# Weights of a step scaled or summed at the end of the step in front, their words made ahead of the second block's probabilities, and the squares spread over four steps

## The chip, the cores and the metric

The kernel runs on one core of one Trainium2 chip. The metric is the device time of one launch in microseconds (us); the time before is the median of three runs. A kernel's profile is one further execution, recorded by the hardware profiler.

## What is computed

The reference mixes two branches of the same 2048 tokens of width 576 with a gate per token:

```python
x = A_x
g = _sigmoid((x * gate_w).sum(-1, keepdims=True))
a = _A_ref(x, A_wq, A_wk, A_wv, A_wo, A_beta)      # 32 heads of 18, 4 segments of 512 tokens
b = (_gelu(x @ w_gate) * (x @ w_up)) @ w_down       # hidden width 4608
return g * a + (1 - g) * b
```

In `_A_ref` each head has, per segment, a causal softmax over 512x512 logits times the values, mixed with a recall from a memory that the segments in front have written. Matrix products are made of two 16-bit words per number, a high word and a low word (the rest that the high word leaves), so that one product of the reference is three on TensorE.

## The kernel before

**Stages.** First the projections q, k, v and the memory recalls are made (to about 205 us). Then come 72 steps `v`, two for each of the 36 slices of 128 hidden columns `f = v // 2`; a slice is taken for the first 1024 tokens at even `v` and for the second 1024 at odd `v`. Last comes the product with wo. Steps 5 to 65 are `paired_step`: beside the feed-forward work of its slice and token half, each does one head of one half of the tokens in attention (`k = v - 2`), as two blocks, `a = 2k` and `b = 2k + 1`. Four steps make a group `fb = v // 4`, with `i4 = v % 4`.

**Order.** TensorE (PE), ScalarE (ACT), VectorE (DVE) and GpSimd (POOL) run their instructions in the order in which the program text issues them (`manual_schedule`). Only the queue of the DMA issues (SP) is ordered by the framework. So an instruction that waits holds up all that stands behind it on its engine.

**A paired step on TensorE** is, in order: the first product into V (`first_product`, words at S3), the product A11 into X, two chains of the group in front (`late(0, 2)`; a chain is six products of 288 columns in `down`, L1051, taken into `acc` by VectorE, L1059), values of the even block (L1005), A22 and G4 into V, `late(2, 4)`, S2 into Y, `late(4, 6)`, in steps with `i4 == 1` the tiny product of `scales` (L234), values of the odd block, `late(6, 8)`, S1, G4, the low rests (L1102), the eight score products of both blocks (L948), A12 and U4 into X, S4 and UG into Y.

**Banks.** The chains, the product of `scales` and four of the score products take turns in two PSUM banks called dn. A new tile takes the bank of the tile before last, and its first instruction waits until that tile's last reader is done. `scales` reads and writes its dn tile with six small VectorE instructions, L236 to L244.

**Weights.** A slice's raw fp32 weights are loaded to `raw` (gate and up) and `rawd` (down). Their sums of squares are made on ScalarE (`squares`, L85), `scales(fb + 1)` turns these into scales on VectorE, and `scales_out` (L250 to L258) finishes them on GpSimd. GpSimd then scales raw weights in place (`scale_g`, L278, `scale_d`, L317) or, a step later, forms their sums and differences (`sums_g`, L299 to L303). `weights_first(fb, i4)` issues these: scaling at `i4` 0 and 2, sums at 1 and 3, and `scale_d` at 2 and 3 as well. ScalarE makes the high words (`weights_high`, L309 and L321) and GpSimd the low words (`weights_low`, L313 and L325). The words of a step's half of a slice are thus used from the next step or the one behind it on; those made at `i4 == 3` are first needed by the first product of the next step.

**Probabilities.** A score piece is taken from PSUM by VectorE with the mask and its row maximum (`put`, L954) into `pf`. `powers` makes the exponentials on ScalarE (L971, L974), `pair_rows` the high words on ScalarE (L984) and the low words on GpSimd (L985, two instructions to a block), and `turn_rows` transposes them by DMA (L991). Block `a` goes through this at the end of its own step, block `b` in the middle of the next step, where its remaining pieces are also taken. `pf` has two buffers, so a piece of block `b` waits until the low words of block `b` of the step in front are made.

**The hidden half.** VectorE adds the partial sums (L1242, L1244), ScalarE applies gelu (L1081; its table has to be loaded again after exponentials), VectorE multiplies (`hidden`, L1073), ScalarE and GpSimd make the words `hh` (L1077, L1078).

Of the kernel before, what the change touches and what calls it, by code (L numbers as in the profile page):

```python
# [18 lines left out]
P = 128  # L19
# [23 lines left out]
def kernel(ctx: ExitStack, tc: tile.TileContext, xs, wqk, wv, wo, wgu, wd, beta, out):  # L43
# [846 lines left out]
    with tc.tile_pool(name="keep", bufs=2, side="right", reuse_waits="tile") as kp, ExitStack() as tail:  # L890
# [226 lines left out]
        def weights_high(fb, i4):  # L1117
            n0 = 2 * fb
            high_g(n0 + 1 + i4 // 2, i4 % 2)
            if i4 >= 2:  # L1120
                high_d(n0 + i4 - 2)

        def weights_low(fb, i4):
            n0 = 2 * fb
            low_g(n0 + 1 + i4 // 2, i4 % 2)
            if i4 >= 2:
                low_d(n0 + i4 - 2)
# [16 lines left out]
        def act_squares(v):  # L1144

            fb, i4 = divmod(v, 4)
            todo = {0: ((fb + 1, 2 * fb, 2),),
                    1: ((fb + 1, 2 * fb + 3, 0), (fb + 1, 2 * fb + 3, 1), (fb + 1, 2 * fb + 1, 2)),
                    2: ((fb + 2, 2 * fb + 4, 0), (fb + 2, 2 * fb + 4, 1))}
            todo = todo.get(i4, ()) if fb else ()  # L1150
            if v == 4:
                todo += (2, 4, 0), (2, 4, 1)
            for b, f, i in todo:
                squares(b, f, i, act_square)
# [22 lines left out]
        def paired_step(v):  # L1177

            f, p = divmod(v, 2)
            fb, i4 = divmod(v, 4)  # L1180
            c, e = 2 * p, 2 * p + 1
            k = v - LAG
            a, b = 2 * k, 2 * k + 1
            late = lambda i, j: chains(fb - 1, range(8 * i4 + i, 8 * i4 + j))
            put = puts.pop(2 * k - 1)
            done = (k - 5) // 4 if i4 == 3 and 0 <= (k - 5) // 4 < H // 2 else None
            low = (k - 6) // 4 if i4 == 0 and 0 <= (k - 6) // 4 < H // 2 - 1 else None
            x1, x2_, t = x16[c], x16[e], xt[p]
            X, Y = bank("G"), bank("U")
            if ends:  # L1190
                end_pair([lambda i=i: put(i) for i in (2, 3)])
            V, g1 = first_product(v), gl_tile()
            dve.tensor_copy(g1, V)
            act_squares(v)
            product(X, f, A11, x1, 0, 4, True)
            put(0)
            dve.tensor_copy(Y, X)
            put(1)
            put(3)
            late(0, 2)  # L1200
            values(2 * k - 4)
            weights_first(fb, i4)
            powers(2 * k - 1)
            pair_rows(2 * k - 1, 0)
            pair_rows(2 * k - 1, 1)
            turn_rows(2 * k - 1)
            weights_high(fb, i4)
            weights_low(fb, i4)
            weights_load(fb, i4)
            product(V, f, A22, x2_, 0, 4)  # L1210
            rest(V, f, G4, x1, (0,))
            late(2, 4)
            if low is not None:
                result_low(low)
            product(Y, f, S2, t, 4, 6)
            g0 = gl_tile()
            dve.tensor_copy(g0, Y)
            late(4, 6)
            if i4 == 1:
                scales(fb + 1)  # L1220
                scales_out(fb + 1)
            values(2 * k - 3)
            normalize(k - 2)
            late(6, 8)
            if i4 == 3:
                load_v(fb + 1)
            product(Y, f, S1, t, 0, 2)
            rest(Y, f, G4, x2_, (0,))
            low_rests(f, (V, G4, x1), (Y, G4, x2_))
            (one, put1), (two, put2) = score(a), score(b)  # L1230
            s0, s1, d0, d1, o = bank("st", 2), bank("st", 2), bank("dn", 2), bank("dn", 2), bank("pv")
            one(0, 0, d1)
            one(1, 64, o[:, : 3 * P])
            one(3, 64, o[:, 3 * P :])
            two(0, 0, s0)
            one(2, 64, d0[:, : 2 * P])
            two(2, 64, d0[:, 2 * P :])
            low_rests(f, (X, U4, x1))
            two(1, 64, s1[:, : 3 * P])
            two(3, 64, s1[:, 3 * P :])  # L1240
            puts[b] = put2
            dve.tensor_tensor(g1, Y, g1, OP.add)  # L1242
            gelu(f, e, g1, g1)
            dve.tensor_tensor(g0, V, g0, OP.add)  # L1244
            gelu(f, c, g0, g0)
            put1(2)
            put2(2)
            product(X, f, A12, x1, 2, 6)
            rest(X, f, U4, x1, (0,))
            hidden(f, c, X, g0)  # L1250
            hidden_pair(f, c, g0)
            put1(0)
            put1(1)
            put1(3)
            product(Y, f, S4, x2_, 2, 6)
            rest(Y, f, UG, x2_)
            hidden(f, e, Y, g1)
            powers(a)
            pair_rows(a, 0)
            pair_rows(a, 1)  # L1260
            turn_rows(a)
            if done is not None:
                result_high(done)
            hidden_pair(f, e, g1)
            load_head(k + 2)
            if i4 == 2:
                load_ob(fb)
# [320 lines left out]
        LAG = 2  # L1588
# [68 lines left out]
```

## Time and profile before

| | |
|---|---|
| median of 3 runs | 1590.53 us (1590.24 to 1590.97) |
| the profiled execution's own time | 1590.79 us |
| its span, first to last instruction | 1589.1 us |
| paired steps, first to last, by the window asked for | 276 to 1406 us |
| in this window: PE busy | 1109.87 of 1130.00 us |
| ACT, POOL, DVE busy there | 941.31, 943.27, 832.42 us |
| granted TensorE clock | 1.00 of full |

A line of the profile has engine, source line, operation, output and inputs; in the timeline the first two numbers are start and length in us, neighbours of one kind are merged (`x6`), and a bracket gives how long the engine had been idle before and what released it. The length of a PE line holds the way through the array, so two matmuls of 512 columns lie about 0.22 us apart though each is shown with 0.38. PE's busy time is therefore no measure of gaps: they are read from starts.

### The profile page before, as it was taken

The page shows a single profiled execution, that of the slowest core. Times are in us where ns is not written, and L with a number is a line of the kernel's source. Part 1 is how long each engine was busy: PE and PEld are TensorE (multiplying, and loading weights), DVE is VectorE, ACT ScalarE, POOL GpSimd, SP SyncE. Part 2 cuts the span into 40 slices and gives each one's busy share as a digit, 9 for nine tenths or more (in the row PEclk, how much of TensorE's full clock was granted, in tenths as well). Part 3 has the DMA queues.
Part 4 walks back from the last instruction along what each step waited for, and adds up shares of the span by engine and source line. Part 5 has one row for each costly group of instructions (what it writes and reads, how often), then busy time and mean ns, then how long its engine had stood idle before and what let it go on. Part 6 is the DMA issues. An engine that isn't in the chain of part 4 may idle for free.

```text
span 1589.1 us, 32678 instructions
## 1 busy us (share of the span) xinstructions
PE 1563.7 (98%) x11902; PEld 937.8 (59%) x11902; DVE 1158.2 (73%) x2995; ACT 1179.7 (74%) x1973; POOL 1225.9 (77%) x1164
## 2 busy tenths in 40 slices
PE   9999999999999999999999999999999999999999
PEld 5665654555555555556555555555555555555577
DVE  6688876777777686777777777777786777775766
ACT  6667648888888787878787888888788888884310
POOL 3445767878888888788888778888878888887774
PEclk9999999999999999999999999999999999999999
DMA  6633346687878696869687778878686879745153
GB/s 222 217 124 115 138 143 107 116 136 121 135 121 146 114 155 118 141 121 141 121 137 130 135 140 123 138 130 140 119 158 121 140 127 144 124 80 142 40 142 98
DMA packets 472305, 209.00 MB, mean 132 GB/s; under 512 B 427600, under 2 KB 437072, under 8 KB 471632
## 3 DMA queue, kind: packets, MB, share of 16 engines
q1 hardware_dynamic: 472144, 206.92, 68.1%
q8 instruction: 93, 1.52, 0.4%
q14 instruction: 68, 0.56, 0.1%
HBM read 90.99 MB, written 27.26 MB: 74 GB/s over the span
## 4 chain that ended last, share of the span: by engine, by line
PE 37%; POOL 26%; ACT 23%; DVE 7%; issue 5%; DMA 2%; SPq 1%; POOLq 0%; ACTq 0%; DVEq 0%
POOL ph L985 8%; PE dn L1051 7%; ACT pf L974 6%; POOL raw L278 6%; PE U L1091 4%; ACT gl L1081 4%; ACT L974 4%; ACT L1081 4%; DVE pf L954 4%; PE G L1091 3%; PE V L1091 3%; POOL rawd L317 3%; POOL hh L1078 3%; PE st L333 3%; DVE gl L1073 2%
## 5 line engine op out<-in xcount | busy, mean ns | idle before, releaser
L985 POOL TENSOR_TENSOR ph<-pf,ph 128x512 f16<-128x512 f32 (+1 forms) x256 | 353.3, 1401 | 181.0 <-ACT ph L984 177.1
L1091 PEld LDWEIGHTS <-pairg 128*128 128x128 f16 x3024 | 283.1, 98 | 335.5 <-POOL pairg L313 27.5
L1051 PE MATMUL dn<-paird,hh 128*128 128x288 f16 x3408 | 465.9, 286 | 0.0
L1051 PEld LDWEIGHTS <-hh 128*128 128x128 f16 x3456 | 333.0, 98 | 124.6 <-DVE pb L244 0.3
L1059 DVE SCALAR_TENSOR_TENSOR acc<-dn,ev,acc 128x288 f32<-128x288 f32 x536 | 264.5, 514 | 120.1 <-PE dn L1051 119.7
L974 ACT ACTIVATE pf<-pf,mb,esc 128x512 f32<-128x512 f32 (+3 forms) x512 | 293.0, 643 | 7.0 <-POOL hh L1078 0.4
L1091 PE MATMUL G<-x,pairg 128*128 128x512 f16 x864 | 212.0, 380 | 0.5 <-DVE gl L1073 0.4
L1091 PE MATMUL U<-xt,pairg 128*128 128x512 f16 x864 | 210.0, 379 | 0.0
L1078 POOL TENSOR_TENSOR hh<-gl,hh 128x512 f16<-128x512 f32 x144 | 174.4, 1213 | 14.7 <-ACT hh L1077 14.7
L313 POOL TENSOR_TENSOR pairg<-raw,pairg 128x640 f16<-128x640 f32 (+2 forms) x144 | 174.4, 1232 | 4.0 <-ACT pairg L309 4.0
L984 ACT ACTIVATE ph<-pf 128x512 f16<-128x512 f32 (+1 forms) x256 | 172.4, 721 | 0.0
L954 DVE CUSTOM_DVE_ANT_0 pf<-dn,mask 128x256 f32<-128x256 f32 (+1 forms) x195 | 95.8, 497 | 87.7 <-POOL ph L985 83.6
L309 ACT ACTIVATE pairg<-raw 128x640 f16<-128x640 f32 (+2 forms) x144 | 89.8, 650 | 78.5 <-POOL raw L303 48.6
L1077 ACT ACTIVATE hh<-gl 128x512 f16<-128x512 f32 x144 | 89.6, 623 | 74.0 <-DVE gl L1073 73.8
L278 POOL TENSOR_SCALAR raw<-raw,sc 128x640 f32<-128x640 f32 x72 | 135.5, 1894 | 0.0
L1091 PE MATMUL V<-xt,pairg 128*128 128x512 f16 x432 | 107.7, 380 | 20.1 <-POOL pairg L313 20.1
L1081 ACT ACTIVATE gl<-gl,sc 128x512 f32<-128x512 f32 x144 | 96.5, 715 | 32.3 <-DVE gl L1383 20.0
L1091 PE MATMUL U<-x,pairg 128*128 128x512 f16 x432 | 107.3, 379 | 0.0
L1091 PE MATMUL V<-x,pairg 128*128 128x512 f16 x432 | 104.8, 378 | 0.0
L954 DVE CUSTOM_DVE_ANT_0 pf<-st,mask 128x512 f32<-128x512 f32 (+2 forms) x195 | 95.1, 512 | 0.0
L1005 PEld LDWEIGHTS <-pt 128*128 128x128 f16 x2560 | 83.3, 96 | 5.4
L1005 PE MATMUL pv<-vt,pt 128*128 128x37 f16 x2560 | 84.3, 179 | 0.0
(311 smaller groups left out, 2671.2 us busy)
## 6 DMA issues: line engine op xcount, KB each, us to landing
raw<-in_wgu_dram SPq DMA_DIRECT2D x36, 640.0 KB
rawd<-in_wd_dram SPq DMA_DIRECT2D x36, 288.0 KB
qk<-stage SPq DMA_DIRECT2D x36, 256.0 KB
qt<-qk SPq DMA_DIRECT2D x128, 72.0 KB
kt<-qk SPq DMA_DIRECT2D x128, 72.0 KB
vp<-vstage SPq DMA_DIRECT2D x16, 296.0 KB
vt<-vp SPq DMA_DIRECT2D x16, 296.0 KB
qt<-qk SPq DMA_DIRECT2D x128, 36.0 KB
```

What stands on the lines that cost most here:

```text
L278: pool.tensor_scalar(r, r, scl[f // 2][0][:, 0:1], None, OP.mult)
L313: pool.tensor_tensor(spot(f, *p, 1), raw_g[f][:, p[0] : p[1]], spot(f, *p, 0), OP.subtract)
L954: dve.tensor_tensor_reduce(prob[a][:, COL[qi] : COL[qi + 1]], outs.pop(i), mask[:, L - (qi + 1) * P :], 1.0, -3e38, OP.add, OP.max, mx[a][ ...
L974: act.activation(r, r, AF.Exp, bias=b[:, qi : qi + 1], scale=esc[:, 0, c : c + 1])
L984: act.activation(h[:, 0, cols], p[:, cols], AF.Copy)
L985: pool.tensor_tensor(h[:, 1, cols], p[:, cols], h[:, 0, cols], OP.subtract)
L1005: pe.matmul(ov, pr[:, 10 * i + COL[qi] // P + kb], v[:, 4 * e + kb, c0 : c0 + VC], start=kb == 0 and i == 0, stop=kb == qi and i == 1)
L1051: pe.matmul(o[:, :NH], hh[:, a, q * P : (q + 1) * P], w[:, b, n * NH : (n + 1) * NH], start=i == 0, stop=i == 5)
L1059: dve.scalar_tensor_tensor(av, o[:, :NH], ev, av, OP.mult, OP.add)
L1078: pool.tensor_tensor(hh[:, 1], t, hh[:, 0], OP.subtract)
L1081: act.activation(t, o, AF.Gelu_apprx_tanh, scale=scl[f // 2][0][:, 2 + c : 3 + c])
L1091: pe.matmul(o, w[:, i, (a + k) * P : (a + k + 1) * P], x[:, b + k], start=start and n == 0, stop=n == 5, skip_group_check=True)
```

## The change

The call of `weights_first` for a step moves to the end of the step in front, behind the words of that step's first hidden half; only step 5 still makes its own call as well. The words (`weights_high`, `weights_low`) go ahead of the odd block's `powers`, `pair_rows` and `turn_rows`. The squares of a group, so far 1, 3, 2 and 0 to a step on ScalarE, become 2, 2, 1 and 1. In steps with `i4 == 1` `scales` goes ahead of `late(4, 6)`. The score products of block `a`'s first piece and of the two third pieces swap their dn banks, and VectorE takes the third piece of block `b` behind the second `hidden` and no longer ahead of the first.

```diff
--- before.py
+++ after.py
@@ -1191,7 +1191,6 @@
                 end_pair([lambda i=i: put(i) for i in (2, 3)])
             V, g1 = first_product(v), gl_tile()
             dve.tensor_copy(g1, V)
-            act_squares(v)
             product(X, f, A11, x1, 0, 4, True)
             put(0)
             dve.tensor_copy(Y, X)
@@ -1199,13 +1198,18 @@
             put(3)
             late(0, 2)
             values(2 * k - 4)
-            weights_first(fb, i4)
+            if v == LAG + 3:
+                weights_first(fb, i4)
+            for w in {0: ((fb + 1, 2 * fb, 2), (fb + 1, 2 * fb + 3, 0)),
+                      1: ((fb + 1, 2 * fb + 3, 0),) * (fb == 1) + ((fb + 1, 2 * fb + 3, 1), (fb + 1, 2 * fb + 1, 2)),
+                      2: ((fb + 2, 2 * fb + 4, 0),), 3: ((fb + 2, 2 * fb + 4, 1),)}[i4]:
+                squares(*w, act_square)
+            weights_high(fb, i4)
+            weights_low(fb, i4)
             powers(2 * k - 1)
             pair_rows(2 * k - 1, 0)
             pair_rows(2 * k - 1, 1)
             turn_rows(2 * k - 1)
-            weights_high(fb, i4)
-            weights_low(fb, i4)
             weights_load(fb, i4)
             product(V, f, A22, x2_, 0, 4)
             rest(V, f, G4, x1, (0,))
@@ -1215,10 +1219,10 @@
             product(Y, f, S2, t, 4, 6)
             g0 = gl_tile()
             dve.tensor_copy(g0, Y)
-            late(4, 6)
             if i4 == 1:
                 scales(fb + 1)
                 scales_out(fb + 1)
+            late(4, 6)
             values(2 * k - 3)
             normalize(k - 2)
             late(6, 8)
@@ -1229,12 +1233,12 @@
             low_rests(f, (V, G4, x1), (Y, G4, x2_))
             (one, put1), (two, put2) = score(a), score(b)
             s0, s1, d0, d1, o = bank("st", 2), bank("st", 2), bank("dn", 2), bank("dn", 2), bank("pv")
-            one(0, 0, d1)
+            one(0, 0, d0)
             one(1, 64, o[:, : 3 * P])
             one(3, 64, o[:, 3 * P :])
             two(0, 0, s0)
-            one(2, 64, d0[:, : 2 * P])
-            two(2, 64, d0[:, 2 * P :])
+            one(2, 64, d1[:, : 2 * P])
+            two(2, 64, d1[:, 2 * P :])
             low_rests(f, (X, U4, x1))
             two(1, 64, s1[:, : 3 * P])
             two(3, 64, s1[:, 3 * P :])
@@ -1244,17 +1248,19 @@
             dve.tensor_tensor(g0, V, g0, OP.add)
             gelu(f, c, g0, g0)
             put1(2)
-            put2(2)
             product(X, f, A12, x1, 2, 6)
             rest(X, f, U4, x1, (0,))
             hidden(f, c, X, g0)
             hidden_pair(f, c, g0)
+            if v + 1 < LAST - 1:
+                weights_first(*divmod(v + 1, 4))
             put1(0)
             put1(1)
             put1(3)
             product(Y, f, S4, x2_, 2, 6)
             rest(Y, f, UG, x2_)
             hidden(f, e, Y, g1)
+            put2(2)
             powers(a)
             pair_rows(a, 0)
             pair_rows(a, 1)
```

On GpSimd the change of order looks like this. Before, from the end of a step with `i4 == 2` into the next: `hh` with the lower number is the first hidden half's word, `ph` the low words of the probabilities, `raw` and `rawd` the weights that are summed and scaled, `pairg` the low words of weights.

```order
L1078 TENSOR_TENSOR hh_7006<-gl,hh_7006 128x512
L930 MEMSET ob 128x288
L299 TENSOR_TENSOR raw<-raw 128x256
L300 TENSOR_TENSOR raw<-raw 128x256
L301 TENSOR_TENSOR raw<-raw 128x256
L302 TENSOR_TENSOR raw<-raw 128x256
L303 TENSOR_TENSOR raw<-raw 128x128
L317 TENSOR_SCALAR rawd<-rawd,sc 128x576
L985 TENSOR_TENSOR ph<-pf,ph 128x512
L985 TENSOR_TENSOR ph<-pf,ph 128x768
L313 TENSOR_TENSOR pairg<-raw,pairg 128x640
L313 TENSOR_TENSOR pairg<-raw,pairg 128x512
```

The same place now, from the first hidden half's word in the step with `i4 == 2`:

```order
L1078 TENSOR_TENSOR hh_6974<-gl,hh_6974 128x512
L299 TENSOR_TENSOR raw<-raw 128x256
L300 TENSOR_TENSOR raw<-raw 128x256
L301 TENSOR_TENSOR raw<-raw 128x256
L302 TENSOR_TENSOR raw<-raw 128x256
L303 TENSOR_TENSOR raw<-raw 128x128
L317 TENSOR_SCALAR rawd<-rawd,sc 128x576
L985 TENSOR_TENSOR ph<-pf,ph 128x512
L985 TENSOR_TENSOR ph<-pf,ph 128x768
L1078 TENSOR_TENSOR hh_7010<-gl,hh_7010 128x512
L930 MEMSET ob 128x288
L313 TENSOR_TENSOR pairg<-raw,pairg 128x640
```

The sums and the scaling have moved from behind the even block's low words and the step's second `hh` to ahead of them, and the two `ph` that stood between the sums and the low words of the weights (those of the odd block) now stand behind the latter.

On TensorE, in a step with `i4 == 1`, the product of `scales` has moved. It now stands behind S2, as a piece of the difference shows (`U<-xt` is S2's last matmul, `dn<-paird` a chain's):

```order
 L1091 LDWEIGHTS pairg
 L1091 MATMUL U<-xt_2240,pairg 128x512
+L234 MATMUL dn<-stat_88,ones 128x10
 L1051 LDWEIGHTS hh_2648
 L1051 MATMUL dn<-paird,hh_2648 128x288
```

and no longer stands between the second of the two chains and the values:

```order
 L1051 LDWEIGHTS hh_2884
 L1051 MATMUL dn<-paird,hh_2884 128x288
-L234 MATMUL dn<-stat_88,ones 128x10
 L1005 LDWEIGHTS pt
 L1005 MATMUL pv<-vt,pt 128x37
```

So one chain now lies between the product of `scales` and the next user of its dn bank, where one chain and twenty products of 37 columns did before.

## Prediction

> **What bounds the kernel now.** I read the page first, then the waits of TensorE, then TensorE's timeline step by step, then the other engines around the one wait found. The page's first part and the list of waits:
>
> ```profile
> PE 1563.7 (98%) x11902; PEld 937.8 (59%) x11902; DVE 1158.2 (73%) x2995; ACT 1179.7 (74%) x1973; POOL 1225.9 (77%) x1164
> PE V L1091 <- POOL pairg L313: 20.1, 15, 1.5
> ```
>
> No engine but PE is near its full span, and PE has one wait of any size: 15 times the first product V waits for a low word of weights from POOL (20.1 us in total). The steps show whether this is all. I take the first low rest of each step (L1102 into V) as its mark; the five marks are of steps with `i4` 0, 1, 2, 3 and 0, and between the last two stands V's stall.
>
> ```profile
> 718.93 0.39 PE L1102 MATMUL V<-x,pairg 64*128 64x512 f16 x1
> 737.39 0.39 PE L1102 MATMUL V<-x,pairg 64*128 64x512 f16 x1
> 755.50 0.39 PE L1102 MATMUL V<-x,pairg 64*128 64x512 f16 x1
> 773.64 0.39 PE L1102 MATMUL V<-x,pairg 64*128 64x512 f16 x1
> 777.87 0.59 PE L1091 MATMUL V<-xt,pairg 128*128 128x512 f16 x2
> 779.99 1.04 PE L1091 MATMUL V<-xt,pairg 128*128 128x512 f16 x4 [1.53 <-POOL pairg L313]
> 793.46 0.39 PE L1102 MATMUL V<-x,pairg 64*128 64x512 f16 x1
> ```
>
> The distances are 18.46 (with the product of scales), 18.11, 18.14 and 19.82. Matmuls of 512 columns lie 0.22 apart within the 1.04 of four, so the first two of V end at 777.87 + 0.43 = 778.30, and the stall costs 779.99 - 778.30 = 1.69: just what the fourth distance has over 18.13. The steps without it are PE at its own pace. Early and late groups differ a little:
>
> ```profile
> 327.07 0.39 PE L1102 MATMUL V<-x,pairg 64*128 64x512 f16 x1
> 346.41 0.39 PE L1102 MATMUL V<-x,pairg 64*128 64x512 f16 x1
> 1367.90 0.39 PE L1102 MATMUL V<-x,pairg 64*128 64x512 f16 x1
> 1387.42 0.39 PE L1102 MATMUL V<-x,pairg 64*128 64x512 f16 x1
> ```
>
> The first group stalls 19.34 - 18.13 = 1.2, the last 19.52 - 18.13 = 1.4. The seven groups of the first 1024 tokens' attention are the first and six like the one at 779.99 (1.7); eight more are like the last. Stalls in all: 1.2 + 6 x 1.7 + 8 x 1.4 = 22.6 us. More than this the change can't gain in the paired steps, as nothing that it moves is PE's own work.
>
> **The weights' early start.** Why V's words are late is seen on POOL, from the first hidden half of the step with `i4 == 2`:
>
> ```profile
> 762.65 1.18 POOL L1078 TENSOR_TENSOR hh<-gl,hh 128x512 f16<-128x512 f32 x1
> 766.47 2.76 POOL L985 TENSOR_TENSOR ph<-pf,ph 128x512 f16<-128x512 f32 x2 [2.65 <-ACT ph L984]
> 769.19 1.17 POOL L1078 TENSOR_TENSOR hh<-gl,hh 128x512 f16<-128x512 f32 x1
> 770.59 0.73 POOL L299 TENSOR_TENSOR raw<-raw 128x256 f32<-128x256 f32 x1
> 774.12 1.73 POOL L317 TENSOR_SCALAR rawd<-rawd,sc 128x576 f32<-128x576 f32 x1
> 775.81 2.77 POOL L985 TENSOR_TENSOR ph<-pf,ph 128x512 f16<-128x512 f32 x2
> 778.53 2.53 POOL L313 TENSOR_TENSOR pairg<-raw,pairg 128x640 f16<-128x640 f32 x2
> 774.18 1.26 ACT L309 ACTIVATE pairg<-raw 128x640 f16<-128x640 f32 x2 [2.71 <-POOL raw L303]
> 776.59 1.28 ACT L1081 ACT_TABLE_LOAD   x1
> 777.88 1.33 ACT L1081 ACTIVATE gl<-gl,sc 128x512 f32<-128x512 f32 x2
> ```
>
> POOL idles 2.65 us, then does `ph`, `hh`, sums (770.59 to 774.12), scaling, the odd `ph`, and only then the low words of which V takes the first, half of 2.53. Now sums and scaling (3.5 + 1.7 = 5.2) begin at 763.8, in the idle time: they end at 769.0, `ph` at 771.8, `hh` at 772.9, with the memset 773.2. ACT can make the high words as soon as it has taken `hh`, well before that, since the sums are done by 767.4; so the low words start about 773.2 and V's first are there at 774.5, against a need at 777.87 + 0.43. That is 3.8 us of room, and the stall goes. Then the rest of POOL's step: low words to 775.7, those of `rawd` (about 1.3) to 777.0, odd `ph` to 779.8 against 778.58 before. The next user of that `ph` is the third piece of block b, which waited 2.91 for it:
>
> ```profile
> 778.61 0.42 DVE L954 CUSTOM_DVE_ANT_0 pf<-dn,mask 128x256 f32<-128x256 f32 x1 [2.91 <-POOL ph L985]
> 761.86 0.75 DVE L1073 SCALAR_TENSOR_TENSOR gl<-U,sc,gl 128x512 f32<-128x512 f32 x1
> 762.32 1.63 PE L1051 MATMUL dn<-paird,hh 128*128 128x288 f16 x12
> ```
>
> It now stands behind the second `hidden`, so the first `hidden` is freed of that wait. What waits for the moved piece is its dn bank, taken by the second chain of the next step. In the step in front, which has no stall, `hidden` ends by 762.6, the piece by 763.05, and the second chain starts at 762.32 + 0.73 = 763.05. That would be tight if nothing else moved. But gelu ends late there only because ACT has weights' words ahead of its table load (776.59 behind 774.18 and the wait for the sums); these now go ahead of the odd block's `powers`, so gelu can follow the adds. I estimate the piece done 1.5 us or more before its bank is wanted, and take nothing for it; without that cover it would cost its lateness in each of 61 steps. ACT's load for a step doesn't change over a group: the squares only level out.
>
> SP's queue gets POOL's events in another order: the load of raw weights goes ahead of the odd transposes. Its condition (the low words made) now comes earlier than the odd `ph`, so nothing behind it is held; nought.
>
> **Scales ahead of two chains.** This is the new wait, in the 16 steps with `i4 == 1`. The rows of one before:
>
> ```profile
> 732.00 1.63 PE L1051 MATMUL dn<-paird,hh 128*128 128x288 f16 x12
> 733.60 0.36 PE L234 MATMUL dn<-stat,ones 128*128 128x10 f32 x2
> 733.82 0.66 PE L1005 MATMUL pv<-vt,pt 128*128 128x37 f16 x20
> 732.27 0.69 DVE L1217 COPY gl<-U 128x512 f32<-128x512 f32 x1 [0.84 <-PE U L1091]
> 732.94 0.52 DVE L1059 SCALAR_TENSOR_TENSOR acc<-dn,ev,acc 128x288 f32<-128x288 f32 x1
> 734.10 0.16 DVE L236 TENSOR_REDUCE z<-dn 128x2 f32<-128x10 f32 x1
> 734.75 0.15 DVE L244 TENSOR_SCALAR pb<-dn 128x4 int32<-128x4 int32 x1
> ```
>
> Two chains take 1.47 (12 products; next at 733.47), so the product of scales and its own small wait cost 733.82 - 733.47 = 0.35. Now PE comes to it at 732.00, spends 0.22 (733.60 to 733.82), runs the first chain to 732.95, and wants the bank of scales for the second. VectorE still has the copy of Y from 732.27, its next instruction 0.67 later: L236 starts at 732.94, and L236 to the end of L244 takes 734.90 - 734.10 = 0.80, to 733.74. How PE answers is in the first paired step, where a chain has waited for this very bank:
>
> ```profile
> 286.90 0.36 PE L234 MATMUL dn<-stat,ones 128*128 128x10 f32 x2
> 287.40 0.16 DVE L236 TENSOR_REDUCE z<-dn 128x2 f32<-128x10 f32 x1
> 288.25 0.15 DVE L244 TENSOR_SCALAR pb<-dn 128x4 int32<-128x4 int32 x1
> 288.46 0.60 PEld L1051 LDWEIGHTS <-hh 128*128 128x128 f16 x6 [0.26 <-DVE pb L244]
> ```
>
> The chain's weight load comes 0.06 behind the end of L244 (288.25 + 0.15 = 288.40). So the second chain starts at 733.80 and not at 732.95: 0.85 of stall. Against before that is 0.22 + 0.85 - 0.35 = 0.72 a step, 16 x 0.72 = 11.5 us. By the hold of the first paired step (287.40 to 288.40, 1.00 and not 0.80) it would be 0.92 a step, 14.7. Were the load itself hidden, it would be 0.1 less than the 0.72, 9.9; a load of a chain takes 98 ns:
>
> ```profile
> L1051 PEld LDWEIGHTS <-hh 128*128 128x128 f16 x3456 | 333.0, 98 | 124.6 <-DVE pb L244 0.3
> ```
>
> The Trainium skill (Perfetto Trace Analysis, Optimizing Scalar/DVE Operations) gives VectorE about 60 ns of busy overhead an instruction in SBUF and 125 in PSUM. By that the six would hold the bank an estimated 0.36 to 0.75 us, and the loss would be down to 7 us smaller. The measured rows stand for the same six instructions, so they decide.
>
> The product also waits for the squares. Those of `i4 == 1` are now two and no longer three; before, the first two began at
>
> ```profile
> 730.32 0.72 ACT L85 ACTIVATE junk<-raw 128x640 bf16<-128x640 f32 x1
> 731.17 0.74 ACT L85 ACTIVATE junk<-raw 128x640 bf16<-128x640 f32 x1
> ```
>
> that is 0.85 apart, so two would end at 732.0, just when PE now comes. They are earlier by what ACT gains in the step in front, where words like the 1.26 at 774.18 stood ahead of gelu and no longer do; I estimate 1 us and take nought, but it is the thinnest cover of all. If it failed, PE would stall by the lateness in 16 steps.
>
> **Sum.** The profiled execution took 1590.79 (span 1589.1). 1590.8 - 22.6 + 11.5 = 1579.7; the median of the runs lies 0.3 below that execution, so 1579.4.
>
> **Rivals.** (1) Scales cost nothing: VectorE gets to them early or the bank isn't the one I take. Then 1590.5 - 22.6 = 1567.9. Against it: VectorE runs in order and stands behind the copy of Y, which waits for S2. 0.09. (2) The third piece of block b, now late, holds its dn bank past the next step's second chain. Its place is the start of every paired step; it decides once the piece ends over 3.3 us behind the first product's start. If it is late by 0.25 us (I take a third of what a chain takes), 61 x 0.25 = 15.3: 1579.4 + 15.3 = 1594.7, slower. For it: 763.05 against 763.05 above; against it: the earlier gelu. 0.06. (3) The stall stays, because the words can't be written earlier: their buffer is held, two slices being all it has. Then only the cost is left: 1590.5 + 11.5 = 1602.0. The Trainium skill (Perfetto Trace Analysis, Optimization Strategy) says that consistent bubbles "can mean there isn't enough SBUF/PSUM for the next tile to be allocated". The row at 774.18 speaks against: ACT waited for the sums (L303), not for a buffer. 0.05.
>
> **The numbers.** My forecast, 1579.4, has 0.76. About 0.04 is left for waits that I don't see and that eat the rest of the gain. About 0.2% (3.2 us) is what a measurement of this kernel can tell from no change: faster 0.76 + 0.09 + 0.01 = 0.86, same 0.03, slower 0.06 + 0.05 = 0.11. The range reaches down to the first rival, 1567, since the forecast alone holds too little. Upward it takes in 14.7 for 11.5 (1582.6) and a loss of 0.05 us a step at the dn bank (3), 1586.
>
> **What would show it.** Right: no wait of V for L313 is left; steps at 18.1 but for `i4 == 1`, which take 19.2; and in these a weight load of L1051 waits about 0.8 for L244. Wrong: the steps with `i4 == 1` still at 18.5 (rival 1); dn waits of L1051 for L954 at the start of all steps (2); V still waiting (3); or PE's product L234 waiting for ACT's L85, which would say that my ACT schedule is late by over 1 us.

## The result, and the profile after

| | before | after |
|---|---|---|
| median | 1590.75 us (1590.24 to 1590.97, 4 runs) | 1600.21 us (1597.82 to 1602.28, 4 runs) |
| the profiled execution's own time | 1590.79 us | 1597.82 us |
| its span | 1589.1 us | 1596.1 us |

The ratio after to before is 1.0059, 95% interval 1.0041 to 1.0078: the change made the kernel slower, where 1579.4 us was forecast. The four runs differ with their mean granted TensorE clock: 0.999, 0.998, 0.996 and 0.996 of full for 1597.82, 1598.33, 1602.09 and 1602.28 us (0.003 of 1600 is 4.8 us). Why the clock moves at all is seen below.

The page's first part and TensorE's waits of after, against 20.1 us for POOL's `pairg` before (columns: us in total, times, longest):

```profile
PE 1562.6 (98%) x11902; PEld 940.4 (59%) x11902; DVE 1171.9 (73%) x2995; ACT 1166.9 (73%) x1973; POOL 1229.9 (77%) x1164
PE dn L1051 <- DVE pb L244: 28.3, 16, 2.1
PEld L1051 <- DVE pb L244: 33.2, 16, 2.4
```

The wait of V for L313 is gone. In its place stands the one wait that the forecast added, 16 times as it said, but it is longer. The marks of the same five steps, in TensorE's timeline of after:

```profile
719.55 0.39 PE L1102 MATMUL V<-x,pairg 64*128 64x512 f16 x1
739.77 0.39 PE L1102 MATMUL V<-x,pairg 64*128 64x512 f16 x1
757.88 0.39 PE L1102 MATMUL V<-x,pairg 64*128 64x512 f16 x1
776.02 0.39 PE L1102 MATMUL V<-x,pairg 64*128 64x512 f16 x1
794.14 0.39 PE L1102 MATMUL V<-x,pairg 64*128 64x512 f16 x1
```

The distances are 20.22, 18.11, 18.14 and 18.12, where before had 18.46, 18.11, 18.14 and 19.82. The last one is healed as forecast; the first, with `scales`, was to be 19.2 and is 20.22.

The timeline of after inside that step shows where this went; all rows are of TensorE, VectorE and GpSimd around the six instructions of `scales`:

```profile
732.61 0.29 PE L234 MATMUL dn<-stat,ones 128*128 128x10 f32 x2
732.75 0.90 PE L1051 MATMUL dn<-paird,hh 128*128 128x288 f16 x6
732.79 2.51 POOL L313 TENSOR_TENSOR pairg<-raw,pairg 128x640 f16<-128x640 f32 x2
733.49 0.16 DVE L236 TENSOR_REDUCE z<-dn 128x2 f32<-128x10 f32 x1
733.68 0.22 DVE L238 TENSOR_SCALAR dn<-x,z 128x4 f32<-128x4 f32 x1
733.82 0.40 DVE L241 TENSOR_SCALAR v<-z 128x2 int32<-128x2 int32 x1
734.13 0.15 DVE L242 TENSOR_SCALAR pb<-dn 128x4 int32<-128x4 int32 x1
734.25 1.08 DVE L243 TENSOR_SCALAR v<-v 128x2 int32<-128x2 int32 x1
735.24 0.15 DVE L244 TENSOR_SCALAR pb<-dn 128x4 int32<-128x4 int32 x1
735.45 0.91 PE L1051 MATMUL dn<-paird,hh 128*128 128x288 f16 x6 [1.80 <-DVE pb L244]
```

The second chain starts 0.06 behind the end of L244, as the prediction had read it from the first paired step. Read from starts, as the prediction counted, it stalls for 1.96 us and not for 0.85: the first chain's six products end at 732.75 + 0.74 = 733.49, and the second starts at 735.45 (the profile's 1.80 is counted from the end of the last product's line). For L236 to the end of L244 take 735.39 - 733.49 = 1.90 us, where before's rows had 0.80. Two of the six are longer than they were: L241 with 0.40 and L243 with 1.08, both on two numbers to a partition, where L242 and L244 take 0.15 for four. They are the two of the six that have all they read and write in SBUF (`v<-z`, `v<-v`). Of the others three read PSUM, and L238 reads SBUF but writes PSUM; its 0.22 is what it takes in every step, before and after. And each of the two ends when one of POOL's two L313 ends: the pair takes 2.51 from 732.79, so the second ends at 735.30, and L243 at 735.33. L243 over the whole execution, by its minimum, median and maximum, in ns, first before, then after:

```profile
L243 DVE TENSOR_SCALAR v<-v x19: 159/170/377, 163.7 to 1478.9; 128x2 int32<-128x2 int32 x19
```

```profile
L243 DVE TENSOR_SCALAR v<-v x19: 158/1077/1080, 164.2 to 1486.0; 128x2 int32<-128x2 int32 x19
```

So over half of all L243, 15 of 19, take about 1.08 and not 0.17. Behind the first paired step, the steps with `scales` take 20.21 to 20.23, but for one of 20.50 and one of 21.90. The longest, in windows of after (columns: length, busy time of PE, PEld, DVE, ACT and POOL, granted clock, DMA share, GB/s):

```profile
1256.00:1257.00 1.00, 0.06 (x1) 0.00 (x0) 0.96 (x5) 1.00 (x3) 1.00 (x2) 1.00 0.46 106
1257.00:1258.00 1.00, 0.14 (x2) 0.12 (x3) 1.00 (x3) 1.00 (x3) 0.72 (x1) 1.00 1.28 287
1259.00:1260.00 1.00, 1.00 (x16) 0.72 (x13) 0.97 (x3) 1.00 (x1) 1.00 (x2) 0.69 0.76 297
1260.00:1261.00 1.00, 1.00 (x6) 0.59 (x4) 0.89 (x5) 0.27 (x1) 1.00 (x1) 0.50 1.00 331
1261.00:1262.00 1.00, 1.00 (x5) 0.59 (x4) 0.48 (x3) 0.00 (x0) 0.77 (x4) 0.50 1.18 104
1262.00:1263.00 1.00, 1.00 (x4) 0.39 (x3) 0.49 (x1) 0.00 (x0) 0.69 (x3) 0.61 1.27 222
```

TensorE stands still from 1256.1 to 1257.9, and from 1259.4 the granted clock is half for some 3.4 us. What is lost is 0.31 + 0.50 + 0.50 + 0.39 = 1.70 us, which is this step's length over 20.21.

### The profile page after: what moved, and what is told of

It is laid out like the page before. It is cut to its first block, busy times and chain, and to the rows that moved or that the text cites. A ratio compares the mean times of both kernels' runs of the same rounds, so it can differ in the third digit from the quotient of the medians.

```text
span 1596.1 us, 32678 instructions
## 1 busy us (share of the span) xinstructions
PE 1562.6 (98%) x11902; PEld 940.4 (59%) x11902; DVE 1171.9 (73%) x2995; ACT 1166.9 (73%) x1973; POOL 1229.9 (77%) x1164
## 3 DMA queue, kind: packets, MB, share of 16 engines
q8 instruction: 93, 1.52, 0.4%
## 4 chain that ended last, share of the span: by engine, by line
PE 89%; DVE 4%; ACT 3%; POOL 2%; issue 1%; DMA 0%; SPq 0%; DVEq 0%; ACTq 0%; POOLq 0%
PE dn L1051 24%; PE U L1091 16%; PE G L1091 11%; PE V L1091 10%; PE pv L1005 4%; PE U L1097 3%; PE st L333 2%; PE G L333 2%; PE dn L342 2%; POOL ph L985 1%; PE V L1102 1%; PE U L333 1%; PE U L1543 1%; ACT pf L974 1%; PE dn L948 1%; PE G L1097 1%
## 5 line engine op out<-in xcount | busy, mean ns | idle before, releaser
L1059 DVE SCALAR_TENSOR_TENSOR acc<-dn,ev,acc 128x288 f32<-128x288 f32 x536 | 264.3, 513 | 162.5 <-PE dn L1051 162.0
L1078 POOL TENSOR_TENSOR hh<-gl,hh 128x512 f16<-128x512 f32 x144 | 167.4, 1164 | 152.0 <-ACT hh L1077 150.3
L313 POOL TENSOR_TENSOR pairg<-raw,pairg 128x640 f16<-128x640 f32 (+2 forms) x144 | 180.2, 1274 | 6.7 <-ACT pairg L309 4.8
L309 ACT ACTIVATE pairg<-raw 128x640 f16<-128x640 f32 (+2 forms) x144 | 85.8, 641 | 20.0 <-POOL raw L303 14.0
L1073 DVE SCALAR_TENSOR_TENSOR gl<-G,sc,gl 128x512 f32<-128x512 f32 x72 | 54.0, 751 | 50.4 <-PE G L1097 42.7
```

What stands on the lines that cost most here:

```text
L313: pool.tensor_tensor(spot(f, *p, 1), raw_g[f][:, p[0] : p[1]], spot(f, *p, 0), OP.subtract)
L1059: dve.scalar_tensor_tensor(av, o[:, :NH], ev, av, OP.mult, OP.add)
L1078: pool.tensor_tensor(hh[:, 1], t, hh[:, 0], OP.subtract)
```

## The experiments

The theory that they test (P, the port): VectorE's instructions from SBUF to SBUF wait for a running instruction of GpSimd, and the change put L313 beside `scales`, so that the hold of the dn bank grew from 0.80 to 1.90 us. Its first rival is that the move of `scales` costs what the prediction priced (0.72 a step) and that another part of the change costs the rest. A second theory (C, the clock) is that waits of TensorE of about 2 us make the granted clock fall. Times below are medians with the lowest and the highest run; ratios are to the kernel before, measured beside each.

**1. `scales` behind the chains again, all else as changed.**

```diff
+            late(4, 6)
             if i4 == 1:
                 scales(fb + 1)
                 scales_out(fb + 1)
-            late(4, 6)
```

> The changed kernel with one part undone: in steps with i4 == 1 scales stands behind late(4, 6) again. My theory (the changed kernel loses its time at the dn bank that the six small instructions of scales hold, 1.95 us of stall in each of 16 steps, and what is left of the change gains the 22.6 us of the V stalls): no wait of L1051 for L244 above 0.3 us, all four steps of a group at 18.1 to 18.7, and 1568 to 1573 us. Rival A (the words and weights moved ahead slow VectorE or GpSimd wherever scales stand, and L244 is only where that shows): the stall goes to another wait of TensorE and the time stays above 1590 us.

Measured: 1569.48 us (1568.64 to 1570.01), ratio 0.9863 [0.9849, 0.9878], clock 1.00. No wait of TensorE over 0.4 us is left in the paired steps, and steps with `scales` take 18.46 as before. The move of `scales` alone turns a gain of 21 us into a loss of 9. Between the two profiled executions lie 1597.82 - 1568.64 = 29.2 us. 15 steps with 20.22 - 18.46 = 1.76 each make 26.4 (in the first paired step the next one gives the loss back, 19.07 here against 18.11), the lowered clock 1.7, and 1.1 lie ahead of the first mark; their cause stays open. A step of 18.74 here stands where after has its 20.50, so that one has nothing to do with the clock: in both, L241 takes 0.28 us longer there than in the other steps.

**2. As 1, and the product of `scales` in a bank of its own.** Its tile comes from the two banks called st and not from dn.

```diff
-    def scales(fb):
+    def scales(fb, o=None):
-        o = spare()
+        o = spare() if o is None else o
...
-                scales(fb + 1)
+                scales(fb + 1, bank("st", 2))
```

> As the run with scales behind late(4, 6), and the product of scales goes to an st bank in place of a dn bank, so that no chain can wait for it. My theory: no wait of TensorE is left in the paired steps, and the step with i4 == 1 has only the product's own 0.2 to 0.35 us more than 18.1; 1566 to 1569 us, at most 4 us less than with the dn bank. Rival A: above 1590 us.

Measured: 1566.19 us (1566.09 to 1566.35), ratio 0.9843 [0.9829, 0.9858]. Steps with `scales` take 18.25: 0.21 less than with the dn bank, 16 x 0.21 = 3.4 us.

**3. The changed kernel, its two instructions from SBUF to SBUF read from PSUM.** The sum `z` is made a second time, into the dn bank, and what L241 and L243 read is taken from there; eight instructions instead of six, the same results. `scales` stays ahead of the chains, and POOL is left as it is.

```diff
         dve.tensor_reduce(z, o[:, :10].rearrange("p (a b) -> p a b", a=2), AX.X, OP.add)
+        zp, vp = o[:, 24:26], o[:, 28:30]
+        dve.tensor_reduce(zp, o[:, :10].rearrange("p (a b) -> p a b", a=2), AX.X, OP.add)
...
-        dve.tensor_scalar(v[:, 0].bitcast(I32), z.bitcast(I32), 1, EXP, OP.logical_shift_right, OP.bitwise_and)
+        dve.tensor_scalar(vp.bitcast(I32), zp.bitcast(I32), 1, EXP, OP.logical_shift_right, OP.bitwise_and)
+        dve.tensor_scalar(v[:, 0].bitcast(I32), vp.bitcast(I32), EXP, None, OP.bitwise_and)
...
-        dve.tensor_scalar(v[:, 1].bitcast(I32), v[:, 0].bitcast(I32), EXP, None, OP.bitwise_xor)
+        dve.tensor_scalar(v[:, 1].bitcast(I32), vp.bitcast(I32), EXP, None, OP.bitwise_xor)
```

> The changed kernel, scales still ahead of late(4, 6); only the two instructions that read and write SBUF alone (L241 at 0.40 us and L243 at 1.08 us beside GpSimd's L313) now read PSUM: the sums z are reduced a second time into PSUM, and v is made from there with one instruction more (eight in place of six, the same results). Theory P (these two wait for an SBUF port that GpSimd's L313 holds): each of the eight takes 0.12 to 0.25 us, the bank is held about 1.1 us in place of 1.9, the stall falls from 1.95 to 1.1 or 1.2, and the time to 1583 to 1588 us. Rival B (L243 is long for another reason: a semaphore of GpSimd, or the two-column shape): the instructions stay long, the hold grows with two more, and the time is 1600 us or more.

Measured: 1583.96 us (1583.06 to 1584.01), ratio 0.9953 [0.9936, 0.9970], clock 1.00. The same place in its timeline (lines below L240 are three further down than in after, so L316 is L313 and L247 is L244):

```profile
728.91 2.51 POOL L316 TENSOR_TENSOR pairg<-raw,pairg 128x640 f16<-128x640 f32 x2
729.61 0.16 DVE L236 TENSOR_REDUCE z<-dn 128x2 f32<-128x10 f32 x1
730.14 0.17 DVE L243 TENSOR_SCALAR dn<-dn 128x2 int32<-128x2 int32 x1
730.35 0.16 DVE L244 TENSOR_SCALAR v<-dn 128x2 int32<-128x2 int32 x1
730.49 0.15 DVE L246 TENSOR_SCALAR v<-dn 128x2 int32<-128x2 int32 x1
730.56 0.15 DVE L247 TENSOR_SCALAR pb<-dn 128x4 int32<-128x4 int32 x1
730.76 0.91 PE L1054 MATMUL dn<-paird,hh 128*128 128x288 f16 x6 [1.00 <-DVE pb L247]
```

POOL's two instructions run across all eight of VectorE, from 728.91 to 731.42, and none of the eight takes over 0.22. The hold is 1.10 us with two instructions more, against 1.90 with two less; the step takes 19.42 and not 20.22. GpSimd's work and the place of `scales` are as in after; what is gone is only that two instructions have all their operands in SBUF. So P is shown. All traces say the same: from the first paired step on, in the eleven in which L241 and L243 work from SBUF to SBUF, they start 184 times while one of GpSimd's sums (L299 to L303) or low words (L313) runs, and end 0.02 to 0.03 us behind its end each time; the other 190 times they take 0.16 to 0.17.

Run 3 also says what the move costs without contention: 19.42 - 18.46 = 0.96 a step with a hold of 1.10; with 0.80 it would be about 0.66, beside the 0.72 of the forecast. The Trainium skill has the rule (SBUF — State Buffer, Who interferes with whom): VectorE and GpSimd share one pair of SBUF ports, forms such as `tensor_scalar` in a mode that uses both ports contend for it, and the one that comes second "fully blocks". The runs agree: L241 and L243 last until L313 ends, and not with PSUM among their operands. In which mode they run, no run shows.

**4. The kernel before, with the move of `scales` alone** (the reverse of the diff of 1, on before).

> The kernel before with one part of the change alone: scales ahead of late(4, 6). The V stalls stay. By my prediction's price of 0.72 us a step: 1590.8 + 11.5 = 1602 us. By theory P, GpSimd is then at the sums (L299 to L303, 0.73 us each, both operands in SBUF), L241 and L243 end only with one of these each, the bank is held 1.8 to 1.9 us and the time is 1615 to 1620 us. If the cost arises only together with the words made ahead (rival A): 1591 to 1595 us.

Measured: 1601.80 us (1601.34 to 1602.14), ratio 1.0067 [1.0052, 1.0082]. TensorE's waits:

```profile
PE V L1091 <- POOL pairg L313: 14.0, 15, 1.1
PE dn L234 <- ACT junk L85: 10.4, 15, 0.7
PE dn L1051 <- DVE pb L244: 3.2, 14, 1.1
```

P's expectation missed. It had the right instructions beside `scales`, the sums with 0.73 us each, but not their place: in 15 of the 16 steps L241 starts only 0.2 us ahead of the end of L299, with which it ends, and L243 starts in the gap of 0.08 us ahead of L300 and takes 0.17 (means of all: 257 and 168 ns). The time is near what the price of 0.72 gave, but by other terms: the product of `scales` waits for the squares on ScalarE, three in this step, as in before. Steps with `scales` take 19.54, 1.08 more than before, 16 x 1.08 = 17.3 us; the steps with V's stall take 19.37 and 19.09 and not 19.8 and 19.52, 14 x 0.43 = 6.0 us less (the first gains nothing), as if a part of V's wait had only moved; 1590.8 + 17.3 - 6.0 = 1602.1 beside 1601.86 in the profiled execution. So the cover that the prediction called the thinnest is thin indeed: without the other parts of the change the product waits 0.7 us a step for the squares, with them it doesn't wait.

**5. The changed kernel, with the hold made longer**: the last of the six instructions is issued nine times and not once, with the same result.

```diff
+        for _ in range(8 if fb > 1 else 0):
+            dve.tensor_scalar(pb[:, 1].bitcast(I32), z4.bitcast(I32), EXP, EXP, OP.bitwise_and, OP.bitwise_xor)
         dve.tensor_scalar(pb[:, 1].bitcast(I32), z4.bitcast(I32), EXP, EXP, OP.bitwise_and, OP.bitwise_xor)
```

> The changed kernel with L244 issued nine times in place of once in the paired steps (the same values each time), which holds the dn bank of scales some 0.6 to 0.9 us longer: the stall in the 16 steps grows from 1.95 to 2.6 to 2.9 us. By length alone that is 16 x 0.75 = 12 us more than the changed kernel's best run, about 1610 us. Theory C (a stall of TensorE of about 2 us or more sometimes lowers its granted clock for some us, and that, at 1.7 us each, is the spread of the changed kernel's runs from 1598 to 1602): the clock falls in most of the 16 groups, the mean granted clock goes below 0.995, and the time to 1620 to 1640 us. Rival (the fall of the clock in the changed kernel has nothing to do with the length of the stall): clock 0.996 to 1.000 as before and 1607 to 1615 us.

Measured: 1642.52 us (1640.13 to 1646.18), ratio 1.0331 [1.0314, 1.0348], clock 0.984. The place of one such wait, and windows of TensorE's waits (columns as above):

```profile
1060.11 1.52 DVE L245 TENSOR_SCALAR pb<-dn 128x4 int32<-128x4 int32 x8
1061.88 0.91 PE L1053 MATMUL dn<-paird,hh 128*128 128x288 f16 x6 [3.36 <-DVE pb L246]
```

```profile
1059.30:1062.72 3.42, 0.84 (x10) 0.70 (x11) 2.67 (x11) 3.40 (x5) 2.81 (x3) 1.00 0.91 222
1062.72:1066.13 3.41, 3.41 (x34) 2.34 (x33) 2.53 (x7) 0.01 (x1) 2.18 (x7) 0.50 0.68 175
752.10:755.52 3.42, 1.68 (x30) 1.46 (x31) 2.56 (x13) 2.57 (x4) 2.81 (x4) 1.00 1.09 297
```

The eight take 1.52 us and the wait grows by as much, from 1.80 to 3.36; I had expected about half of that, so the time lies above the range of C as well as of its rival. Taken with what it did measure, 16 x 1.56 = 25.0 us of the 1642.4 - 1597.8 = 44.6 between the profiled executions are the longer wait, and 19.6 are not: behind the first paired step, 4 steps with `scales` take 21.79 (20.22 + 1.57) and 11 take 23.28 to 24.32, and behind the wait of each of the 11, and of the first, the windows show a lowered clock. So C holds: behind a wait of 1.0 us (run 3) the clock fell in none of 16 steps, behind 1.8 in 1 of 16, behind 3.4 in 12 of 16.

Whether a fall follows goes with a wait's place on a fixed raster. In these traces each stretch at half clock lasts 3.413 us or twice that (the one at the program's end apart) and starts a whole multiple of 3.413 us from the others (in run 5 at 287.89 and next at 366.40, which is 23 x 3.413 later). Cut by this raster, each of run 5's 12 waits with a fall leaves TensorE idle for 1.91 us or more in the piece just ahead of the fall, as from 1059.30 above (3.42 - 0.84 = 2.58); the four without a fall are split over two pieces with at most 1.86 in either, as the one with 3.42 - 1.68 = 1.74 from 752.10, behind which the clock stays at 1.00. In after the one wait with a fall lies in one piece, with 1.81 idle; eight others do so too, with 1.78 to 1.80 and no fall. So 1.8 us, a little over half a piece, is about where it turns. It is no sharp limit: in run 7 the clock stays up behind pieces with as much as 2.07 idle.

The Trainium skill (TensorE: Matmul & The Clock Gate, HAM oscillation) warns of idle gaps over about 3.4 us; the one at 1256 was 1.8 long, so here the measurement goes beyond the rule. The length at half clock, 3.4 us, is that of the window that the Trainium skill gives (TensorE: Matmul & The Clock Gate, Part 1: 3413 ns).

**6. The kernel before, with the early weights alone.** Only the call of `weights_first` moves, to behind the words of the step's first hidden half.

```diff
-            weights_first(fb, i4)
+            if v == LAG + 3:
+                weights_first(fb, i4)
             powers(2 * k - 1)
...
             hidden_pair(f, c, g0)
+            if v + 1 < LAST - 1:
+                weights_first(*divmod(v + 1, 4))
             put1(0)
```

> The kernel before with one part of the change alone: a step's scaling or sums at the end of the step in front. Words, scales, squares, banks and the third piece stay as before. By my reading of GpSimd's queue the sums and scaling fill its idle time of 2.65 us and the low words of V's weights come 1 us ahead of their need even behind the odd block's ph: no wait of V for L313, 1568 to 1572 us. Rival (the words must go ahead of the odd block's probabilities as well): the V stall stays in part, 0.3 to 1.2 us a group, 1573 to 1587 us.

Measured: 1568.00 us (1567.81 to 1568.20), ratio 0.9859 [0.9845, 0.9874]. No wait of V is left, and the steps take 18.45, 18.11, 18.13 and 18.12. The gain over the profiled before is 1590.79 - 1567.83 = 23.0 us, against the 22.6 worked out for the stall: all that the change could gain at V comes from this one part. L241 and L243 take 0.16 beside an idle GpSimd here: the early weights alone don't put L313 beside `scales`.

**7. The kernel before, with the words alone ahead of the odd probabilities** (`weights_high` and `weights_low` ahead of `powers`, as in the change's diff, `weights_first` at its old place).

> The kernel before with another part alone: the words of weights ahead of the odd block's probabilities, while scaling and sums stay in the step's own middle. V's words are then there in time, but ScalarE stands at the high words until GpSimd has the sums (774.1 in the step shown) and the odd exponentials, their words and gelu come behind it, about 3 us later than before: TensorE then waits for hidden's G bank in most steps. Over 1620 us. Rival (ScalarE has the room): 1568 to 1575 us.

Measured: 1817.44 us (1815.26 to 1818.51), ratio 1.1426 [1.1409, 1.1443], clock 0.967: over 1620, as expected, and by far. The waits of VectorE and of TensorE:

```profile
DVE pf L954 <- POOL ph L985: 316.0, 61, 7.0
PE G L1091 <- DVE gl L1073: 178.0, 62, 4.7
```

The words of weights that are scaled or summed only in this step hold up the odd block's probabilities behind them; its third piece waits for their low words in each of the 61 steps (before: 45 waits, 83.6 us in all), and `hidden` behind it on VectorE. The lowered clock is a part of the time, 0.033 of 1817, an estimated 60 us. This part is only to be had together with the early weights.

**8. Run 2 without the spread squares and without the late third piece** (both as in before; the dn banks of the score products too).

> The version with the product of scales in an st bank behind late(4, 6), and two further parts of the change undone: squares as before (1, 3, 2, 0 to a step) and the third piece of block b with its banks as before. What is left is the early scaling and sums, the words ahead of the odd block's probabilities and the st bank. If the two parts carry nothing once scales stand late: 1566 to 1567 us, as that version's 1566.2. If the third piece's wait for the odd ph still holds up hidden, or the three squares of i4 == 1 the product of scales: 1570 us or more, with the wait in the row of L1073 or L234.

Measured: 1572.01 us (1571.90 to 1572.22), ratio 0.9885 [0.9870, 0.9899]: 5.8 us slower than run 2. The steps behind those with `scales`, from mark to mark, take 18.43 and not 18.11 (15 times), and the third and fourth paired step 18.49 and 19.52 and not 18.14 and 18.11. Which of the two parts it was is for run 10 to say.

**9. The kernel before with two edits alone: the early weights of 6 and the bank of 2.**

> The kernel before with two edits alone: an odd step's weights scaled or summed at the end of the step in front (its words first there), and the scales' product in a bank of its own among those of the state, where it neither waits for nor holds the bank of the chains; scales at their old place behind late(4,6), squares and third piece of block b as before. Theory that these two edits are all that the best version needs: 1565 to 1567.5 us, no wait of VectorE for POOL's low words, steps with scales at 18.2 to 18.3. Rival, by which the third piece, the banks or the spread squares earn something by themselves: 1570 to 1574, steps that compute neither scales nor words at 18.4 or more.

Measured: 1564.39 us (1564.09 to 1564.60), ratio 0.9834 [0.9818, 0.9851], the fastest of all and a little below the range of its theory. Its steps take 18.25, 18.12, 18.14 and 18.11. It lies 1.8 us below run 2, and the steps say where: they are alike within 0.02 but for the second paired step, 18.13 here and 19.41 there, and a later one, 18.12 and 18.28. In the second paired step run 2 pays for the words ahead of the odd probabilities: the step ahead of it still makes its own sums, ScalarE idles 4.46 us at the high words until they are done, gelu starts at 294.79 and not at 291.70, and TensorE's product G waits for `hidden` (0.68 us, the only wait of that step; run 9 has none). So words ahead of the odd probabilities, spread squares and the late third piece together earn nothing that two edits don't have.

**10. Run 2 with the squares as in before, third piece late.**

```diff
             dve.tensor_copy(g1, V)
+            act_squares(v)
...
-            for w in {0: ((fb + 1, 2 * fb, 2), (fb + 1, 2 * fb + 3, 0)),
...
-                squares(*w, act_square)
```

> The best version so far (1566.2 us: scales behind late(4,6), their product in a bank of the state) with the squares issued as before, the third piece of block b late as in the changed kernel. If the squares carry the 5.8 us that the run without both parts lost: 1571 to 1573, steps before a scale step at 18.4. If the third piece and its bank carry them: 1566 to 1567, all steps as in the best version.

Measured: 1570.29 us (1570.26 to 1570.56), ratio 0.9873 [0.9858, 0.9887]. The squares carry 4.1 of the 5.8 us, since the 15 steps of 18.43 are there again, and the third piece with its bank 1.7, in the third and fourth paired step; so neither expectation holds alone. The squares' part is P once more. The timeline of run 10 and that of run 2, at `scales`:

```profile
724.25 2.52 POOL L313 TENSOR_TENSOR pairg<-raw,pairg 128x640 f16<-128x640 f32 x2 [0.39 <-ACT pairg L309]
726.07 0.72 DVE L241 TENSOR_SCALAR v<-z 128x2 int32<-128x2 int32 x1
728.60 0.94 DVE L1059 SCALAR_TENSOR_TENSOR acc<-dn,ev,acc 128x288 f32<-128x288 f32 x2
728.82 0.39 PE L1102 MATMUL V<-x,pairg 64*128 64x512 f16 x1
729.17 0.37 PE L948 MATMUL dn<-kt,qt 54*128 54x512 f16 x1
730.12 1.47 PE L1091 MATMUL G<-x,pairg 128*128 128x512 f16 x6
```

```profile
724.83 0.29 DVE L241 TENSOR_SCALAR v<-z 128x2 int32<-128x2 int32 x1
726.92 0.93 DVE L1059 SCALAR_TENSOR_TENSOR acc<-dn,ev,acc 128x288 f32<-128x288 f32 x2
727.58 0.39 PE L1102 MATMUL V<-x,pairg 64*128 64x512 f16 x1
727.80 0.38 PE L948 MATMUL dn<-kt,qt 54*128 54x512 f16 x1
728.56 0.82 PE L1091 MATMUL G<-x,pairg 128*128 128x512 f16 x3
```

With three squares ahead of them on ScalarE the words come later, and L313 ends at 726.77, in the middle of `scales`. L241 ends just there (726.79), after 0.72 us and not 0.29; the chains' reader L1059 ends that much later, and the first score product of TensorE, which takes its bank, starts 729.17 - 728.82 = 0.35 behind its mark, where run 2 has 727.80 - 727.58 = 0.22. With the other score products behind it, TensorE's next product G starts 1.30 behind the mark and not 0.98: the 0.32 of the longer step. In run 9, which keeps the old squares, the words stay behind the odd probabilities, POOL stands idle beside `scales`, and L241 and L243 take 0.16 each.

## Why the prediction was wrong

**The step that failed** is a size: "L236 to the end of L244 takes 734.90 - 734.10 = 0.80". The mechanism, the place and the 16 times were as forecast: the product ahead of both chains, the bank held by the six instructions, the weight load 0.06 behind L244, the start of L236 0.67 behind the copy of Y (0.61 in after). But the duration was carried over from a place where POOL did other work. The prediction worked out POOL's new order for the step with `i4 == 3`, where the stall was, and named the low words' new start there; it did not do the same for `i4 == 1`, where two moves together put L313 (2.51 us) beside the six instructions: the words went ahead of the odd probabilities, and `scales` ahead of the chains. With the first move alone (run 1) L241 meets only the last 0.3 us of L313. The bounds, 9.9 to 14.7, came from holds of 0.80 and 1.00, both beside GpSimd's shorter sums. That duration fed the term of 11.5 us. By the marks, which have the 22.6 us of V's stalls back as forecast, the term measured 27.6 us: 15 steps at 1.76, 0.95 in the first paired step, and 0.28 more in the step of 20.50; the clock took 1.7 beside it. With the hold of 1.90 the same sum gives 16 x (0.72 + 1.10) = 29.1 in place of 11.5, and 1590.8 - 22.6 + 29.1 = 1597.3; the profiled execution took 1597.82, 1.7 of it by the clock. The steps themselves show 1.76 and not 1.82, as the product of `scales` takes 0.14 of TensorE (732.61 to 732.75) and not 0.22.

The trace of before could have told. The 0.20 between the two holds is P already: in the first paired step L243 takes 0.38 us and ends at 288.34, beside L303, which ends at 288.32. And in the step shown POOL's sums stood beside the six, and L241 ends with one of them, 734.64 against 734.61:

```profile
733.88 0.73 POOL L300 TENSOR_TENSOR raw<-raw 128x256 f32<-128x256 f32 x1
734.43 0.21 DVE L241 TENSOR_SCALAR v<-z 128x2 int32<-128x2 int32 x1
```

And L241's spread over that execution was wide for an instruction of two numbers, 0.158 to 0.956 us:

```profile
L241 DVE TENSOR_SCALAR v<-z x19: 158/205/956, 162.7 to 1478.7; 128x2 int32<-128x2 int32 x19
```

**The clock** was not among the terms. It explains why the median of the four runs lies 2.4 us above the profiled execution, and 1.7 us within that; that the other three runs lost more of it is read from their mean clock alone.

**The early weights** were right: 22.6 us worked out, 23.0 measured (run 6). The low words even start earlier than forecast: 773.2 against a mark of 773.64 was the estimate, 772.61 against a mark of 776.02 is the trace, 3.0 us sooner within the step.

```profile
772.61 2.53 POOL L313 TENSOR_TENSOR pairg<-raw,pairg 128x640 f16<-128x640 f32 x2
763.28 0.41 DVE L954 CUSTOM_DVE_ANT_0 pf<-dn,mask 128x256 f32<-128x256 f32 x1
764.70 1.63 PE L1051 MATMUL dn<-paird,hh 128*128 128x288 f16 x12
```

**The late third piece** was right: it ends at 763.69, and the second chain starts at 764.70 + 0.73 = 765.43, so 1.7 us of room stand where 1.5 were estimated. **SP's queue** cost nothing that a wait shows. **The squares** kept their cover in the changed kernel, with no wait of L234 for L85; run 4 shows what it is worth, 0.7 us a step, and run 10 that they matter for a reason that the prediction didn't have.

**The rivals.** None of the three came true. The first, `scales` for nothing at 1567.9, is what undoing the move gives (run 1, 1569.5). The third gave nearly the measured time, 1602.0, by luck: no stall of V stayed, and the Trainium skill's remark on consistent bubbles and too little buffer space (Perfetto Trace Analysis, Optimization Strategy) did not apply; run 6 healed the bubble by order alone, with no buffer more.

## What to carry to other kernels

The duration of an instruction from SBUF to SBUF on VectorE (here `tensor_scalar` on two numbers a partition) belongs to the place where it was measured: when a change moves it, or moves GpSimd's work, look up what GpSimd will run beside it, and let it last until that ends if it starts while that runs. That matters most for small instructions that hold something others wait for; operands in PSUM made the hold shorter here (run 3), and a bank of its own, with `scales` behind the chains, took it away from them (runs 2 and 9). When a change has several parts, price the one that adds a wait apart from the one that removes one: here one call moved (run 6) had the whole gain at V, and another move gave more than all of it back.

## What the runs showed of the hardware

An instruction of two numbers a partition, 0.16 us by itself, took up to 1.08 us on VectorE while GpSimd ran a subtraction of 128x640 or 128x512, and 0.15 to 0.17 with its operand in PSUM; in all 184 cases in which it started while GpSimd ran such a subtraction or a sum of weights, it ended 0.02 to 0.03 us behind that. The granted TensorE clock went to half for 3.413 us, or twice that, behind single waits of 1.8 us (1 of 16) and of 3.4 us (12 of 16), and never behind waits of 1.0; the falls lie on a raster of 3.413 us, and in run 5 they came where at least 1.91 us of one of its pieces was idle and not where at most 1.86 was.
